# The high parts of K loaded by casting transfers on GpSimd's queue, in an attention and two-layer kernel on one core

## The chip, the cores and the metric

The kernel runs on one core of a Trainium2 chip. The metric is the device time of one execution in microseconds (us), as the median of several runs. Traces come from the hardware profiler, for one execution each.

## The reference

The program computes attention with pooled queries and feeds the result through two perceptron layers. Cut to what matters:

```
batch, n_heads, seq, head_dim = (2, 8, 1152, 64)
q_pool = q.reshape(B, H, S // 2, 2, D).mean(axis=3)
scores = scale * np.matmul(q_pool, k.transpose(0, 1, 3, 2))      # 576 x 1152 a head
attn = softmax(scores); x = np.matmul(attn, v)                   # 16 heads
x -> (1152, 512)
h = x @ w_in; g = softplus(h); x = g @ w_out                     # 512 -> 2048 -> 512
xn = rmsnorm(x); silu(xn @ w_gate) * (xn @ w_val) @ w_out        # 512 -> 1536 -> 512
```

All inputs and outputs are 32-bit floats. The change touches only how K comes to the score product.

## The kernel before

TensorE multiplies operands of a rounded 32-bit type (fp32r) in one pass. To keep the precision of the product, Q and K are each split into a high part, the value rounded to fp32r, and a low part, the value minus its high part; scores are sums of products of the parts.

The 16 heads are worked as eight pairs, `pb` 0 to 7. For each pair `prep` loads raw K of both heads, transposed, into the tile `kr`: 128 partitions (64 of the first head, 64 of the second) by 1152 positions. From `kr` it makes three things:

- `kk` of each head (two tiles, A and B): the high part of the head on 64 partitions and its low part on the other 64. The high part is one cast of 64x1152 (line 635), on VectorE or ScalarE; the low part is three subtractions of 64x384 (line 638), on VectorE or GpSimd, each of which reads `kr` and the high part.
- `kh` of the pair: the high part of both heads, one cast of 128x1152 (line 646). It serves the pair's last score product, for the last 64 rows of both heads at once.

Pair 0 (`first`) does the casts in three pieces of 384 positions, as they land. `kk` has two sets of tiles, for even and odd pairs, so that a pair's tiles are free once the pair two before has done its last scores. `kr` and `kh` have one tile each: `kr` is loaded anew when all its readers are done, and `kh` is written anew when the last scores of the pair before have read it.

Q goes beside it: the two halves that are pooled are summed into `qs` (`sum_q`, on VectorE or, after pair 0, on GpSimd), rounded to `qhA` or `qhB` (`round_q`, VectorE or ScalarE), and the low parts `qlA` and `qlB` and `qm` come from VectorE.

Per pair there are five row blocks `x`, four of 128 rows and one of 64. For each, `qk` puts scores into PSUM `s` (line 677), VectorE takes the maximum (`nm`, line 691), ScalarE the exponentials and their sums (`p`, line 693), TensorE transposes `p` through the PSUM tile `t` (line 712) and VectorE or ScalarE copies it to `pt` (helper lines 334 and 336), and TensorE multiplies with V (line 755). In pairs 1 to 6, block `x` = 1 is transposed by VectorE and 16 small transfers on SyncE's queue instead (lines 733 and 738). Beside attention, the first weights of the perceptron layers are decoded and split on ScalarE, VectorE and GpSimd (tiles `areaKF`, `areaKR`).

The order on each engine is written by a planner, `Plan`. Every `op` has options (an engine and a cost in us each), the buffers that it reads and writes, and `lat`, the time from the end of a transfer's issue to its landing. The order on TensorE is that of the program. `run` is a list scheduler: of the operations that could start first it takes the one that is due first, with its cheapest engine, and each engine's queue is then in the order of planned starts. A queue is worked strictly in order, so an instruction that waits holds back those behind it. Loads go on SyncE's queue (`load`). In the planner `dve(n, True)` is VectorE's fast copy, and `port` marks operations that it keeps apart from GpSimd's.

Of the kernel before, what the change touches and what calls it, by code (L numbers as in the profile page):

```python
# [21 lines left out]
B, H, S, D = 2, 8, 1152, 64  # L22
# [14 lines left out]
KB = S // N  # L37
# [43 lines left out]
class Plan:  # L81
# [68 lines left out]
    def op(self, opts, fn, r=(), w=(), lat=0.0, after=(), hurry=0.0):  # L150
        o = Op()
        o.fn, o.opts, o.lat, o.hurry = fn, opts, lat, hurry
        o.deps, o.after, o.succ = set(), set(after), []
        o.n = len(self.ops)
        for keys, writes in ((r, False), (w, True)):
            for b, part in keys:
                assert b.live, "a freed buffer"
                o.deps |= self.before(b, part, writes)
        for keys, writes in ((r, False), (w, True)):
            for b, part in keys:  # L160
                (b.writers if writes else b.readers).setdefault(part, []).append(o)
                if not b.ops or b.ops[-1] is not o:
                    b.ops.append(o)
        o.deps.discard(o)
        self.ops.append(o)
        if opts[0][0] == "PE":
            self.pe.append(o)
        return o
# [106 lines left out]
def dve(n, fast=False, psum=False):  # L275
    t = 0.157 + n / (1920 if fast else 960)
    return ("DVE", t) if psum else ("DVE", t, 1)


def act(n, sbuf=True):  # L280
    return "ACT", n * 0.00096 + 0.15 if sbuf else n * 0.00085 + 0.155


def pool(n):
    return "POOL", 0.05 + n * 0.00275
# [3 lines left out]
def body(ctx: ExitStack, tc: tile.TileContext, kT, qT, v, w1, w1o, wg, wv, w2o, rg, outM, outR):  # L289
    nc = tc.nc  # L290
# [3 lines left out]
    op = plan.op  # L294
# [32 lines left out]
    def ring(which, tag, shape, dtype=F32, bufs=1):  # L327
        b = plan.ring(tag, bufs, sb(which, tag, shape, dtype, bufs))
        owned[which].append(b)
        return b  # L330

    def copy(e, out, in_):
        if e == "ACT":
            nc.scalar.copy(out, in_)  # L334
        else:
            engines[e].tensor_copy(out, in_)  # L336
# [6 lines left out]
    def load(out, src, kb, w, queue="SP", lat=2.2, hurry=0.0):  # L343
        q = nc.sync if queue == "SP" else nc.scalar
        o = op([(queue, 0.6 + max(0, kb / 220 - 0.6))], lambda e: q.dma_start(out=out(), in_=src), w=w, lat=lat, hurry=hurry,
               after=issued[queue][-1:] if len(issued[queue]) < 10 else ())
        issued[queue].append(o)
        return o
# [195 lines left out]
    for z in range(2):  # L544
        for h in range(2):
            c = NF * P + (D if h == 0 else 0)
            op([dve(D)], lambda e, b=qx[z][h][0], c=c: copy(e, b()[:, c:c + D], zero), w=[(qx[z][h][0], "z")])
            r = slice(h * D, h * D + D)
            c = D - h * D
# [4 lines left out]
    def prep(pb):  # L554
        s = st[pb]
        n = PAIRS[pb][0] * H + 2 * PAIRS[pb][1]
        first = pb == 0
        s["kk"], s["v"] = [], []
        s["q"] = qx[pb % 2]
        kr = ring("e", "kr", [P, S])  # L560
        qr, qs = [], []
        kcuts = [(c, slice(c * N, c * N + N), N) for c in range(KB)]
        f = NF * P

        def load_q(h, c, queues=("SP", "SP")):
            cut = slice(0, 2 * P) if c == 0 else slice(2 * P, 2 * SQ) if c == 1 else slice(0, 2 * SQ)
            for z in range(2):
                parts = [(qr[h], (x, z)) for x in range(2) if c in (x, None)]
                load(lambda z=z: qr[h]()[z * D:z * D + D, cut], qT[n + h][:, cut], (cut.stop - cut.start) // 4, parts, queues[z], hurry=0.0 if first else EARLY)

        for h in range(2):
            qr.append(ring("a", "p1", [P, 2 * SQ], F32, 2) if first and h else ring("e", "qr", [P, 2 * SQ]))
            qs.append(ring("a", "O", [P, SQ], F32, 2) if first and h else ring("e", "qs", [P, SQ]))
        if first:
            load_q(0, 0, ("SP", "ACTQ"))
        pairs = kT[n:n + 2].rearrange("a d s -> (a d) s")
        if first:
            for c, cut, m in kcuts:
                load(lambda cut=cut: kr()[:, cut], pairs[:, cut], 192, [(kr, c)], "SP" if c else "ACTQ", (2.0, 3.1, 2.7)[c])
            load_q(1, 0)  # L580
        else:
            load(kr, pairs, 576, [(kr, None)], hurry=EARLY)
        for h in range(2):
            load_q(h, 1 if first else None)
            vt = ring("ea"[pb % 2], f"v{h}{pb % 2}", [P, CK, D])
            s["v"].append(vt)
            load(vt, v[n + h], 288, [(vt, None)])

        def round_q(h, key, x, m, i):
            qh, ql = s["q"][h]  # L590
            o = slice(x, x + m)
            op([dve(m, True), act(m)], lambda e: scale16(e, qh()[:, o], qs[h]()[:, i]), r=[(qs[h], None)],
               w=[(qh, k) for k in key])
            op([dve(m)], lambda e: nc.vector.scalar_tensor_tensor(
                out=ql()[:, o], in0=qs[h]()[:, i], scalar=0.0625, in1=qh()[:, o], op0=ALU.mult, op1=ALU.subtract),
               r=[(qs[h], None)] + [(qh, k) for k in key], w=[(ql, k) for k in key])

        def sum_q(h, part, a, m):
            o = slice(a, a + m)
            i = a if part == 0 else a + P  # L600
            j = i + (P if part == 0 else SQ - P)
            op([dve(m)] if first else [dve(m), pool(m)], lambda e: tt(
                e, qs[h]()[:, o], qr[h]()[:, i:i + m], qr[h]()[:, j:j + m], ALU.add), r=[(qr[h], (part, z)) for z in range(2)],
               w=[(qs[h], part)])

        kh = s["kh"] = ring("a", "kh", [P, S], F32R)

        def last_q(h):
            qh, low = s["q"][h][0], qm[pb % 2]
            x = f if h == 0 else f + D  # L610
            r = slice(h * D, h * D + D)
            op([dve(D, True), act(D)], lambda e: scale16(e, qh()[:, x:x + D], qs[h]()[:, f:]), r=[(qs[h], None)], w=[(qh, "e")])
            op([dve(D)], lambda e: nc.vector.scalar_tensor_tensor(
                out=low()[r, h * D:h * D + D], in0=qs[h]()[r, f:], scalar=0.0625, in1=qh()[r, x:x + D],
                op0=ALU.mult, op1=ALU.subtract), r=[(qs[h], None), (qh, "e")], w=[(low, ("e", h))])

        for h in range(2):
            kk = ring("ea"[pb % 2], f"kk{h}{pb % 2}", [P, S], F32R)
            s["kk"].append(kk)
            hi, lo = slice(h * D, h * D + D), slice(D - h * D, P - h * D)  # L620
            if first:
                sum_q(h, 0, 0, P)
                round_q(h, ("m0",), 0, P, slice(0, P))
                for c, cut, m in kcuts:
                    op([dve(m, True), act(m)], lambda e, kk=kk, hi=hi, cut=cut: copy(e, kk()[hi, cut], kr()[hi, cut]),
                       r=[(kr, c)], w=[(kk, ("h", c))])
                    op([dve(m)], lambda e, kk=kk, hi=hi, lo=lo, cut=cut: tt(
                        e, kk()[lo, cut], kr()[hi, cut], kk()[hi, cut], ALU.subtract),
                       r=[(kr, c), (kk, ("h", c))], w=[(kk, ("l", c))])
            else:  # L630
                sum_q(h, 0, 0, P)
                for x in range(2):
                    sum_q(h, 1, P + x * (SQ - P) // 2, (SQ - P) // 2)
                round_q(h, ("m0", "m1"), 0, f, slice(0, f))
                op([dve(S, True), act(S)], lambda e, kk=kk, hi=hi: copy(e, kk()[hi], kr()[hi]),
                   r=[(kr, None)], w=[(kk, ("h", c)) for c in range(KB)])
                for c, cut, m in kcuts:
                    op([dve(m), pool(m)], lambda e, kk=kk, hi=hi, lo=lo, cut=cut: tt(
                        e, kk()[lo, cut], kr()[hi, cut], kk()[hi, cut], ALU.subtract),
                       r=[(kr, None), (kk, ("h", c))], w=[(kk, ("l", c))])  # L640
        for h in range(2):
            if first:
                sum_q(h, 1, P, SQ - P)
                round_q(h, ("m1",), P, f - P, slice(P, f))
            last_q(h)
        op([dve(S, True), act(S)], lambda e: copy(e, kh(), kr()), r=[(kr, None)], w=[(kh, None)])
        s["den"] = ring("a", "den", [P, 2 * NF + 1], F32, 2)
        s["O"] = ring("a", "O", [P, SQ], F32, 2)

# [853 lines left out]
    for which, name in (("soft", "softplus"), ("silu", "silu_and_others")):  # L1503
        before = {"soft": "exp", "silu": "soft"}[which]
        first = op([("ACT", 1.3)], lambda e, name=name: nc.scalar.preload_act_table_set(name))
# [63 lines left out]
```

## Time and profile before

| | |
|---|---|
| median of three runs | 656.72 us (656.21 to 656.9) |
| the profiled execution's own time | 656.31 us |
| its span, first to last instruction | 654.5 us |
| mean granted clock of TensorE | 0.997 |

The execution's own time is that of the run in which the trace was taken; the span leaves out 1.8 us around the first and last instruction. Attention lies in the first 236 us or so of the span, the two perceptron layers behind it. In the rows, PE is TensorE's matmuls and PEld its weight loads, DVE is VectorE, ACT ScalarE, POOL GpSimd and SPq the issuing side of SyncE's queue. Instructions that only issue a transfer are not counted as busy time. L334 and L336 are one helper that copies or casts on ScalarE and on VectorE, and L339 is one that adds or subtracts, so that the tile's name tells what is done.

### The profile page before, as it was taken

The page shows a single profiled execution, that of the slowest core. Times are in us where ns is not written, and L with a number is a line of the kernel's source. Part 1 is how long each engine was busy: PE and PEld are TensorE (multiplying, and loading weights), DVE is VectorE, ACT ScalarE, POOL GpSimd, SP SyncE. Part 2 cuts the span into 40 slices and gives each one's busy share as a digit, 9 for nine tenths or more (in the row PEclk, how much of TensorE's full clock was granted, in tenths as well). Part 3 has the DMA queues.
Part 4 walks back from the last instruction along what each step waited for, and adds up shares of the span by engine and source line. Part 5 has one row for each costly group of instructions (what it writes and reads, how often), then busy time and mean ns, then how long its engine had stood idle before and what let it go on. Part 6 is the DMA issues. An engine that isn't in the chain of part 4 may idle for free.

```text
span 654.5 us, 11104 instructions
## 1 busy us (share of the span) xinstructions
PE 641.6 (98%) x4376; PEld 546.8 (84%) x4376; DVE 496.3 (76%) x741; ACT 399.4 (61%) x648; POOL 117.2 (18%) x131
## 2 busy tenths in 40 slices
PE   8999999999999999999999999999999999999997
PEld 7988889898998888888888888887788888888786
DVE  7888878898989877798877585669887787875320
ACT  4878788887887786556655654355464546563311
POOL 0442365445451310000000000000000100020000
PEclk8999999999999999999999999999999999999999
DMA  7643565656374530133231101300533231310102
GB/s 188 185 127 82 132 156 153 146 144 166 99 203 104 176 126 1 70 126 127 77 126 56 64 3 65 124 5 0 193 130 118 75 129 66 129 65 1 64 1 80
DMA packets 25026, 66.78 MB, mean 102 GB/s; under 512 B 5327, under 2 KB 6286, under 8 KB 24974
## 3 DMA queue, kind: packets, MB, share of 16 engines
q1 hardware_dynamic: 24462, 65.68, 33.0%
q8 instruction: 34, 0.56, 0.3%
q10 hardware_dynamic: 512, 0.40, 0.2%
q14 instruction: 18, 0.15, 0.1%
HBM read 56.59 MB, written 2.39 MB: 90 GB/s over the span
## 4 chain that ended last, share of the span: by engine, by line
PE 90%; DVE 5%; SPq 2%; DMA 1%; ACT 1%; issue 1%; ACTq 0%; DVEq 0%
PE s L870 24%; PE s L677 11%; PE t L755 10%; PE s L1371 9%; PE t L712 7%; PE t L870 4%; PE s L937 3%; PE s L938 3%; PE s L936 3%; PE t L1371 3%; PE t L957 2%; PE s L957 2%; PE t L983 2%; SPq L738 1%; DMA kr<-in_kT_dram 1%; PE s L983 1%
## 5 line engine op out<-in xcount | busy, mean ns | idle before, releaser
L691 DVE TENSOR_REDUCE nm<-s 128x1 f32<-128x1152 f32 x72 | 96.4, 1350 | 12.0 <-PE s L677 11.5
L693 ACT ACTIVATE p<-s,nm 128x1152 f32<-128x1152 f32 x72 | 88.0, 1223 | 17.8 <-DVE nm L691 15.6
L712 PE MATMUL t<-ident,p 128*128 128x128 f32 x468 | 70.4, 280 | 3.1 <-DVE pt L336 1.0
L334 ACT COPY pt<-t 128x512 f32<-128x512 f32 (+2 forms) x105 | 53.4, 523 | 24.7 <-PE t L712 20.6
L755 PE MATMUL t<-pt,v 128*64 128x128 f32 (+1 forms) x1224 | 67.0, 263 | 0.0
L334 ACT CAST areaKR<-areaKF 128x512 fp32r<-128x512 f32 (+1 forms) x56 | 48.7, 877 | 28.8 <-PE t L1371 17.0
L755 PEld LDWEIGHTS t<-pt,v 128*64 128x64 f32 x1224 | 59.6, 137 | 6.9 <-issue 5.8
L712 PEld LDWEIGHTS t<-ident,p 128*128 128x128 f32 x468 | 52.7, 140 | 14.7 <-issue 3.4
L870 PE MATMUL s<-areaMR,areaKR 128*128 128x512 f32 x192 | 48.5, 392 | 0.0
L339 POOL TENSOR_TENSOR kk<-kr,kk 64x384 fp32r<-64x384 f32 x40 | 40.8, 1045 | 39.2 <-ACT kk L334 36.5
L415 DVE SCALAR_TENSOR_TENSOR areaKF<-areaKF 128x1024 int32<-128x1024 int32 (+1 forms) x38 | 44.3, 1169 | 4.1 <-ACT areaKF L404 3.6
L870 PE MATMUL s<-areaKR 128*128 128x512 f32 x180 | 46.8, 398 | 0.1
L334 ACT CAST areaLR<-areaKF 128x1024 fp32r<-128x1024 f32 (+1 forms) x31 | 28.0, 910 | 26.1 <-PE s L1371 15.5
L339 DVE TENSOR_TENSOR areaKR<-areaKF,areaKR 128x1024 fp32r<-128x1024 f32 (+1 forms) x37 | 39.3, 1076 | 6.0 <-ACT areaKR L334 5.8
L339 DVE TENSOR_TENSOR areaKF<-areaKF 128x256 f32<-128x256 f32 (+1 forms) x92 | 41.2, 479 | 1.4 <-ACT areaKF L1010 0.4
L870 PEld LDWEIGHTS s<-areaMR,areaKR 128*128 128x128 f32 x192 | 35.4, 188 | 7.2
L404 ACT ACTIVATE areaKF<-areaKF 128x1024 f32<-128x1024 f32 (+1 forms) x38 | 39.8, 1053 | 0.3 <-DMA areaKF<-in_w_dram 0.3
L870 PEld LDWEIGHTS s<-areaKR 128*128 128x128 f32 x180 | 32.6, 188 | 7.2 <-ACT s L334 0.3
L336 DVE COPY pt<-t 128x512 f32<-128x512 f32 (+2 forms) x49 | 31.2, 650 | 9.3 <-PE t L712 8.5
L870 PE MATMUL s<-areaKR,areaLR 128*128 128x512 f32 x144 | 37.6, 400 | 0.5 <-DVE areaKR L339 0.5
L1072 POOL TENSOR_TENSOR n<-n,power 128x4 f32<-128x4 f32 (+1 forms) x3 | 3.1, 1029 | 175.1 <-DVE n L1070 175.1
L677 PE MATMUL s<-kk,qhA 128*128 128x384 f32 x120 | 31.3, 366 | 1.6 <-DVE kk L339 1.6
(269 smaller groups left out, 1431.0 us busy)
## 6 DMA issues: line engine op xcount, KB each, us to landing
areaKF<-in_w_dram SPq DMA_DIRECT2D x16, 512.0 KB, 4.2
areaKF<-in_w1o_dram SPq DMA_DIRECT2D x16, 512.0 KB, 4.4
qr<-in_qT_dram SPq DMA_DIRECT2D x28, 288.0 KB, 4.5
areaKF<-areaKF SPq DMA_DIRECT2D x96, 72.0 KB, 2.1
areaKF<-in_wg_dram SPq DMA_DIRECT2D x12, 512.0 KB, 3.9
areaKF<-in_wv_dram SPq DMA_DIRECT2D x12, 512.0 KB, 4.6
areaKF<-in_w2o_dram SPq DMA_DIRECT2D x12, 512.0 KB, 3.3
v<-in_v_dram SPq DMA_DIRECT2D x16, 288.0 KB, 3.6
```

Source lines behind the costliest of these rows:

```text
L334: nc.scalar.copy(out, in_)
L336: engines[e].tensor_copy(out, in_)
L339: engines[e].tensor_tensor(out=out, in0=in0, in1=in1, op=o)
L404: o = op([act(n)], lambda e, x0=x0, x1=x1: nc.scalar.activation(out=word(1, x0, x1).bitcast(F32), in_=word(1, x0, x1).bitcast(F32), scale= ...
L415: op([dve(n)], lambda e, x0=x0, x1=x1: nc.vector.scalar_tensor_tensor(out=word(1, x0, x1), in0=word(1, x0, x1), scalar=3, in1=word(0, x0, ...
L677: nc.tensor.matmul(sc()[:, c, :N], lhsT=q()[:, cut], rhs=k()[:, c * N:(c + 1) * N], start=(i == 0), stop=(i == len(todo) - 1))
L691: u["mx"] = op([dve(S, psum=True)], lambda e: nc.vector.tensor_reduce(out=nm(), in_=sc()[:, :, :N], axis=AX.XY, op=ALU.max, negate=True), ...
L693: o = op([("ACT", 1.42)], lambda e: nc.scalar.activation(out=pr(), in_=sc()[:, :, :N], func=AF.Exp, bias=nm(), accum_out=s["den"]()[:, col ...
L712: nc.tensor.transpose(t()[:, i * P:(i + 1) * P], pr[:, c * P:(c + 1) * P], ident)
L755: nc.tensor.matmul(t()[h * D:h * D + D, :n], lhsT=s["v"][h]()[:, c, :], rhs=rhs, start=(c == 0), stop=(c == CK - 1))
L870: nc.tensor.matmul(bank(), lhsT=a(k), rhs=b(k), start=start and k + i == 0, stop=stop and k + i == 3, skip_group_check=seeded)
L1371: nc.tensor.matmul(out[m](), lhsT=w, rhs=g(), start=j + i == 0, stop=last and j == js[-1] and i == 2)
```

## The change

For pairs 1 to 7, the high part of each head's `kk` and the pair's `kh` are no longer cast from `kr`. Each is read again from K in main memory by a transfer on GpSimd's queue, whose destination has the type fp32r, so that the transfer casts. The planner is told 1.2 us on GpSimd for the issue and 4.0 us until it lands. `kr` is still loaded for the low parts, which still wait for the high parts. Pair 0 keeps its casts.

```diff
@@ -632,8 +632,8 @@
                 for x in range(2):
                     sum_q(h, 1, P + x * (SQ - P) // 2, (SQ - P) // 2)
                 round_q(h, ("m0", "m1"), 0, f, slice(0, f))
-                op([dve(S, True), act(S)], lambda e, kk=kk, hi=hi: copy(e, kk()[hi], kr()[hi]),
-                   r=[(kr, None)], w=[(kk, ("h", c)) for c in range(KB)])
+                op([("POOL", 1.2)], lambda e, kk=kk, hi=hi, h=h: nc.gpsimd.dma_start(out=kk()[hi], in_=kT[n + h]),
+                   w=[(kk, ("h", c)) for c in range(KB)], lat=4.0)
                 for c, cut, m in kcuts:
                     op([dve(m), pool(m)], lambda e, kk=kk, hi=hi, lo=lo, cut=cut: tt(
                         e, kk()[lo, cut], kr()[hi, cut], kk()[hi, cut], ALU.subtract),
@@ -643,7 +643,10 @@
                 sum_q(h, 1, P, SQ - P)
                 round_q(h, ("m1",), P, f - P, slice(P, f))
             last_q(h)
-        op([dve(S, True), act(S)], lambda e: copy(e, kh(), kr()), r=[(kr, None)], w=[(kh, None)])
+        if first:
+            op([dve(S, True), act(S)], lambda e: copy(e, kh(), kr()), r=[(kr, None)], w=[(kh, None)])
+        else:
+            op([("POOL", 1.2)], lambda e: nc.gpsimd.dma_start(out=kh(), in_=pairs), w=[(kh, None)], lat=4.0)
         s["den"] = ring("a", "den", [P, 2 * NF + 1], F32, 2)
         s["O"] = ring("a", "O", [P, SQ], F32, 2)
```

## Rows read from the trace of the kernel before

**Rows 1.** The page, busy time, share of the span and instructions of each engine.

```profile
PE 641.6 (98%) x4376; PEld 546.8 (84%) x4376; DVE 496.3 (76%) x741; ACT 399.4 (61%) x648; POOL 117.2 (18%) x131
```

**Rows 2.** Windows, us busy (instructions): PE, PEld, DVE, ACT, POOL; clock, DMA share, GB/s.

```profile
87.00:115.00 28.00, 27.79 (x303) 25.42 (x302) 21.75 (x28) 23.23 (x40) 14.39 (x16) 1.00 0.62 160
115.00:143.20 28.20, 27.88 (x302) 25.36 (x302) 24.68 (x35) 23.74 (x40) 12.02 (x14) 1.00 0.55 137
143.20:171.30 28.10, 27.97 (x304) 25.34 (x302) 25.01 (x34) 23.85 (x42) 15.53 (x17) 1.00 0.54 140
171.30:199.50 28.20, 27.88 (x302) 25.31 (x302) 24.75 (x36) 22.64 (x39) 16.08 (x18) 1.00 0.65 175
...
240.00:654.50 414.50, 408.41 (x1968) 335.76 (x1966) 291.35 (x449) 209.31 (x320) 21.61 (x17) 1.00 0.21 75
```

**Rows 3.** Waits of all engines, 18 to 236 us: us, times, longest.

```profile
PEld t L712 <- DVE pt L336: 2.4, 6, 0.6
...
PE t L712 <- DVE pt L336: 1.0, 3, 0.3
...
PEld t L712 <- ACT O L334: 0.5, 1, 0.5
...
PE t L712 <- ACT pt L334: 0.2, 1, 0.2
```

**Rows 4.** Tile kr: ns minimum/median/maximum, first and last start, forms.

```profile
L339 POOL TENSOR_TENSOR kk<-kr,kk x40: 992/1004/1457, 25.0 to 198.5; 64x384 fp32r<-64x384 f32 x40
L334 ACT CAST kk<-kr x16: 508/1150/1157, 4.9 to 193.4; 64x1152 fp32r<-64x1152 f32 x13, 64x384 fp32r<-64x384 f32 x3
L345 SPq DMA_DIRECT2D kr<-in_kT_dram x9: 327/515/1237, 1.4 to 185.1; - x9
...
L334 ACT CAST kh<-kr x6: 1157/1161/1167, 37.0 to 205.9; 128x1152 fp32r<-128x1152 f32 x6
L336 DVE CAST kh<-kr x2: 750/886/1021, 17.5 to 61.6; 128x1152 fp32r<-128x1152 f32 x2
...
DMA to landing us min/median/max: 3.2/4.3/5.6
```

**Rows 5.** Timeline, raw K of pair 6: start us, us, engine, line, operation, tiles.

```profile
157.47 0.52 SPq L345 DMA_DIRECT2D kr<-in_kT_dram  x1
...
168.79 0.74 DVE L336 CAST kk<-kr 64x1152 fp32r<-64x1152 f32 x1
...
169.76 5.53 POOL L339 TENSOR_TENSOR kk<-kr,kk 64x384 fp32r<-64x384 f32 x5 [2.25 <-PE t L712]
...
176.99 0.77 PE L677 MATMUL s<-kk,qhA 128*128 128x384 f32 x3
```

**Rows 6.** The page, transfers by source: count, KB each, median us to landing.

```profile
v<-in_v_dram SPq DMA_DIRECT2D x16, 288.0 KB, 3.6
```

**Rows 7.** Timeline around the load of raw K in pair 2's time.

```profile
71.33 0.47 SPq L345 DMA_DIRECT2D kr<-in_kT_dram  x1
...
76.34 1.15 ACT L334 CAST kk<-kr 64x1152 fp32r<-64x1152 f32 x1 [1.01 <-DMA kr<-in_kT_dram]
77.39 1.21 ACT L693 ACTIVATE p<-s,nm 128x1152 f32<-128x1152 f32 x1
...
78.75 0.44 PE L677 MATMUL s<-kk,qhB 128*128 128x384 f32 x1 [0.67 <-ACT p L693]
```

**Rows 8.** Timeline, end of pair 3 and first scores of pair 4.

```profile
115.32 2.93 POOL L339 TENSOR_TENSOR kk<-kr,kk 64x384 fp32r<-64x384 f32 x3 [3.46 <-ACT kk L334]
...
115.89 0.68 PE L677 MATMUL s<-kh,qm 128*128 128x384 f32 x3
...
118.60 1.07 POOL L339 TENSOR_TENSOR qs<-qr 128x224 f32<-128x224 f32 x2 [0.35 <-POOL kk L339]
...
121.31 0.69 DVE L594 SCALAR_TENSOR_TENSOR qlB<-qs,qhB 128x512 fp32r<-128x512 f32 x1
...
122.62 0.77 PE L677 MATMUL s<-kk,qhB 128*128 128x384 f32 x3
```

## The prediction

> **What bounds the kernel now.** The profile's busy line comes first: TensorE is busy for 98% of the span, VectorE for 76%, ScalarE for 61%, GpSimd for 18% [rows 1]. A change that only lightens VectorE and ScalarE can therefore win nothing but the time in which TensorE waits for them. The change touches attention alone, which lies in the first 236 us or so, and the windows by pair show how close to full TensorE is there: in pairs 3 to 6 it is busy 27.79 to 27.97 us of 28.0 to 28.2, while VectorE has 21.75 to 25.01 us and ScalarE 22.64 to 23.85 us of work in the same time [rows 2]. A matmul's end is modelled, so part of that busy time may be hidden waiting, but not much. After 240 us the two perceptron layers run with TensorE busy 408.41 us of 414.5 [rows 2]; nothing of K is left there, and I cost that stretch at no change.
>
> The waits of TensorE in attention (18 to 236 us) are the second view. Its matmul row waits visibly six times over for ScalarE or VectorE, 3.3 us in all, from 1.0 us for copies out of PSUM by VectorE down to 0.2 us [rows 3]. Its weight-load row, which shows idle time that the modelled ends hide, names the same two engines in six larger entries (copies of transposed scores 2.4 and 0.7, exponentials 2.3 and 1.1, copies of the output 0.9 and 0.5): 7.9 us [rows 3]. These 3.3 and 7.9 us bound what faster help could return.
>
> **What the casts cost, and what goes.** Seven pairs lose three casts each. The rows of the tile that holds raw K give them: 13 casts of 64x1152 on ScalarE at 1.15 us (15.0 us), one on VectorE at 0.74 [rows 5]; six of 128x1152 on ScalarE at 1.16 us (7.0 us), and of VectorE's two the one at 1.02 us (the 0.75 us one belongs to pair 0, which keeps it) [rows 4]. Sum: 22.0 us off ScalarE and 1.8 us off VectorE, 23.8 us, or 3.4 us a pair.
>
> They are not on TensorE's path by themselves. What they do is fill slots: in pairs 3 to 6 the two engines together have 189.7 us of work in 2 x 112.5 us, which leaves 35.3 us free [rows 2]. Without the casts (4 x 3.4 = 13.6 us) 48.9 us are free. I take the waits of TensorE for these engines to shrink as the free time grows, to 35.3/48.9 = 72% of what they are. That gives back 28% of 3.3 us = 0.9 us at the least and 28% of 7.9 us = 2.2 us at the most; I take the middle, **1.5 us**. This proportion is an estimate of mine, not something a row shows.
>
> **What the casts held up.** The low part of K (raw minus high, three pieces a head, mostly on GpSimd at 1.0 us each [rows 4]) had to wait for a cast to find a slot. In pair 5's time raw K for pair 6 was issued at 157.47, the first cast came at 168.79, and the five subtractions on GpSimd ended at 175.3, 1.7 us ahead of the pair's first score matmul at 176.99 [rows 5]. Afterwards the high part can be fetched as soon as the tile of two pairs ago has been read, some 20 us before it is needed; a load of 576 KB lands in 3.2 to 5.6 us [rows 4] and one of 288 KB in 3.6 us [rows 6], so the transfer is hidden by that lead. If it were not, each head's subtractions would start up to 5.6 us later than raw K, and the 1.7 us of margin would go. The tile of raw K is also free sooner: its last reader was the whole-pair cast, which could come after the next pair had begun. In pair 2 the load of raw K stood in SyncE's queue until 71.33, its cast ran 76.34 to 77.49, an exponential queued behind it on ScalarE, and TensorE stood still for 0.67 us until 78.75 [rows 7]. That stall should go; it is one of the 3.3 us above and is not counted again.
>
> **What comes in.** 21 issues on GpSimd's queue. The trace has no transfer issued there, so the price is bounded by rows: the same tile's issues on SyncE take 0.33 to 1.24 us [rows 4], and GpSimd's own work over the same 64x1152 elements takes 2.93 us in three pieces (115.32, [rows 8]). I take 1.24 us, the longest issue of this tensor, since an issue writes no 64x1152 elements. That is 3.7 us a pair (1.0 to 8.8 us) on an engine with 12.0 to 16.1 us of counted work in 28 [rows 2]; even the dear end fits, at 24.9 us, so by throughput it costs nothing. What hides it is GpSimd's idle time; where it would not be hidden is the first rival below.
>
> Traffic: two heads of 288 KB and one pair of 576 KB are 1,152 KB (1.18 MB) a pair, 42 GB/s over 28 us, on 137 to 175 GB/s that now take 0.54 to 0.65 of the transfer engines [rows 2]. At the same rate per share that adds 0.13 to 0.17, up to about 0.8. Nothing saturates; I cost it at zero, and at the landing times above if transfers bunch.
>
> Waits: the transfer for a whole pair's high part may start only when the last score matmuls of the pair before have read the old one (115.89 plus 0.68, [rows 8]). It stands in GpSimd's queue, and what is queued behind it are the sums of Q for the next pair and the subtractions for raw K. It is needed a pair later, some 27 us.
>
> **Sum.** 656.31 us for the profiled execution, minus 1.5, plus 0: 654.8 us. The median of the runs is 656.72, 0.41 above that execution, so the forecast is **655.2 us**, 0.23% below the median.
>
> **A rule against it.** GpSimd shares a port to the memory with VectorE; here a subtraction of K that takes GpSimd 0.99 us at best takes up to 1.46 us [rows 4]. The Trainium skill (SBUF — State Buffer, section "SBUF: two separate sides", the box on DVE blocking a DMA) says that a transfer issued from GpSimd has its descriptors written by that engine, which is locked out while VectorE runs a fast-mode copy: 620 ns alone became about 3100 ns there. No run here shows that yet. By it an issue would take 3.1 us, an estimate from that page, 9.3 us a pair, and the sum would still hold by throughput, but the next rival would decide.
>
> **Rivals.**
>
> *GpSimd comes late with the sums of Q* (slower). At the end of each pair three transfers become ready at once: the next pair's whole high part and both heads for the pair after. In pair 3 that moment is 116.57. GpSimd then sums Q at 118.60, VectorE finishes the last sum, rounds, and ends the low part at 122.00; TensorE uses it at 122.62 [rows 8]. So three issues have 2.03 us before the sums and 0.62 us of margin behind them: free up to 2.65/3 = 0.88 us each. At 1.24 us they make TensorE 1.07 us late, in six pairs 6.4 us; with the 1.5 us gained, 661.6 us. At 2.93 us each it is 6.1 us a pair and the time near 690 us. For it: the sums now start as soon as their tile is free. Against it: the planner charges 1.2 us for the issue, may place the sums on VectorE, and the subtractions that fill 115.32 to 118.25 now [rows 8] move to an earlier time. It decides as soon as an issue takes more than the 1.2 us which the order was planned with and the sums stand behind it.
>
> *The casts were in the gaps* (no change). ScalarE and VectorE wait for TensorE far more than it waits for them, the planner fills gaps with casts, and most of TensorE's waits are the latency of maximum, exponential and transposition, which stays: 656.3 to 657.0 us. For it: six visible waits in 218 us; against it: the stall at 78.75 is behind a cast.
>
> *More comes back.* Raw K leaves SyncE's queue ahead of the small transfers, low parts are ready well ahead, and the copies out of PSUM are spread over two less busy engines, so that half to three quarters of the 7.9 us return, 4 to 6 us: 650.7 to 652.7 us. For it: the 7.9 us; against it: TensorE is nearly full.
>
> **How the numbers follow.** Forecast 0.40 (its own range 654.5 to 655.8, 2.2 and 0.9 us below the median), rival one 0.25, rival two 0.23, rival three 0.12. From no change a measurement of this kernel can tell about 0.2%, 1.3 us. The forecast lies across that bound: two thirds of it below (0.28), one third within (0.12). Faster: 0.28 + 0.12 = 0.40. Same: 0.12 + 0.23 = 0.35. Slower: 0.25. The range takes in rival two, most of rival three, and rival one with the issue at 1.24 us, but not its dear end: 651.5 to 662 us.
>
> **What would show it.** Right: no casts from raw K after pair 0; ScalarE about 22 us less busy; 21 issues on GpSimd of 1.0 to 1.3 us; subtractions ending over 5 us ahead of the next pair's scores; the PSUM copies' and exponentials' entries in the waits of TensorE shorter, and pairs 3 to 6 at 27.6 to 27.9 us. Wrong: issues of 2 us or more with subtractions or sums of Q behind them, TensorE waiting for the low part of Q or K at a pair's start, pairs over 28.5 us; or pairs of the same length as now in spite of the free engines.

## The result, and the profile after

The changed kernel takes **664.88 us** (median of four runs, 664.01 to 666.36) against 656.60 for the kernel before on the same chip. The ratio is 1.0126, 95% interval [1.011, 1.0142]: slower by 8.3 us, where 1.5 us less were forecast, and above the range, which ended at 662. The profiled execution took 664.01 us.

The busy line and the transfer rows of the page of the changed kernel (count, KB each, median us from issue to landing):

```profile
PE 642.0 (97%) x4376; PEld 546.9 (83%) x4376; DVE 494.3 (75%) x735; ACT 383.3 (58%) x637; POOL 127.5 (19%) x148
...
q1 hardware_dynamic: 24462, 65.68, 32.4%
q0 software_dynamic: 2128, 8.26, 5.4%
...
kk<-in_kT_dram POOLq DMA_DIRECT2D x14, 288.0 KB, 6.9
...
kh<-in_kT_dram POOLq DMA_DIRECT2D x7, 576.0 KB, 5.1
```

ScalarE has 16.1 us less to do than in [rows 1], VectorE 2.0. So the casts are gone, and yet TensorE, with the same work, needs 7.7 us more of span.

The same windows as [rows 2], moved with the pairs (pairs 3 to 6, then the stretch behind attention):

```profile
89.60:119.80 30.20, 27.86 (x304) 25.44 (x303) 22.28 (x31) 20.38 (x38) 19.09 (x23) 1.00 0.79 176
119.80:150.60 30.80, 28.38 (x302) 25.27 (x302) 26.81 (x37) 19.50 (x36) 11.36 (x15) 1.00 0.71 178
150.60:178.60 28.00, 27.79 (x303) 25.35 (x302) 24.18 (x31) 23.67 (x44) 17.71 (x21) 1.00 0.71 183
178.60:207.50 28.90, 28.19 (x304) 25.36 (x303) 24.93 (x32) 20.27 (x38) 13.03 (x17) 1.00 0.79 200
247.80:662.20 414.40, 408.28 (x1968) 335.72 (x1966) 291.81 (x449) 209.45 (x320) 22.00 (x17) 1.00 0.20 75
```

The perceptron stretch is the same to 0.1 us. The loss lies in attention, and not evenly: two pairs last 30.2 and 30.8 us, the others about as long as before. The share of the transfer engines has risen by 0.14 to 0.17, to 0.71 to 0.79, as the prediction added up.

From TensorE's timeline of every kernel, the start of the first score matmul and the length of each pair, from the last score matmuls (kh) of the pair before to its own, in us. Each row is the one execution that was traced; for tiny and half that was the slowest of ten (659.25 and 660.21 us, where their medians are 657.99 and 658.41). The experiments below say what each kernel is.

| kernel | first score | pair 0 | 1 | 2 | 3 | 4 | 5 | 6 | 7 |
|---|---|---|---|---|---|---|---|---|---|
| before | 6.10 | 26.06 | 26.94 | 28.82 | 27.97 | 28.21 | 28.09 | 28.20 | 32.87 |
| changed | 8.98 | 26.65 | 26.95 | 27.94 | 30.16 | 30.84 | 27.98 | 28.84 | 32.70 |
| tiny | 7.16 | 26.66 | 26.92 | 27.96 | 28.13 | 29.02 | 28.82 | 28.67 | 32.71 |
| half | 7.25 | 26.67 | 26.96 | 27.95 | 29.73 | 29.29 | 27.99 | 28.65 | 32.68 |
| pair1_cast | 5.67 | 26.16 | 26.95 | 35.72 | 29.01 | 31.54 | 29.27 | 28.38 | 32.56 |
| tiny1 | 5.83 | 27.06 | 26.95 | 27.97 | 28.97 | 32.51 | 29.23 | 30.11 | 32.56 |
| before_bytes2 | 5.90 | 26.28 | 26.95 | 31.58 | 27.99 | 29.99 | 28.11 | 28.88 | 32.86 |
| in_place | 5.89 | 26.07 | 26.94 | 29.04 | 28.20 | 33.10 | 28.07 | 28.71 | 32.85 |

The changed kernel against before: +2.88 at the start, +0.59 in pair 0, -0.88 in pair 2, +2.19 in pair 3, +2.63 in pair 4, +0.64 in pair 6, the rest within 0.2; in all 7.8 us. Three places make it up, and one gives something back (pair 2, whose stall of 0.67 us at 78.75 in [rows 7] is gone).

**The start.** ScalarE and TensorE of the kernel before:

```profile
4.95 1.58 ACT L334 CAST kk<-kr 64x384 fp32r<-64x384 f32 x3 [0.94 <-DMA kr<-in_kT_dram]
...
6.10 0.44 PE L677 MATMUL s<-kk,qhA 128*128 128x384 f32 x1 [0.58 <-DVE kk L339]
```

GpSimd, ScalarE and TensorE of the changed kernel:

```profile
1.43 1.26 POOL L635 DMA_DIRECT2D kk<-in_kT_dram  x2
...
7.89 0.51 ACT L334 CAST kk<-kr 64x384 fp32r<-64x384 f32 x1 [4.37 <-DMA kr<-in_kT_dram]
...
8.98 0.41 PE L680 MATMUL s<-kk,qhA 128*128 128x384 f32 x1 [3.09 <-DVE kk L339]
```

Nothing holds pair 1's two transfers, so GpSimd issues them at 1.43 us, beside the first pieces of raw K, which pair 0 needs at once. Those land late, and the first scores start 2.9 us later.

**Pair 3.** GpSimd, SyncE, VectorE, TensorE:

```profile
91.52 0.61 POOL L649 DMA_DIRECT2D kh<-in_kT_dram  x1 [1.05 <-PE s L680]
92.12 1.06 POOL L635 DMA_DIRECT2D kk<-in_kT_dram  x2
...
90.49 1.40 SPq L345 DMA_DIRECT2D qr<-in_qT_dram  x2
...
99.37 0.39 DVE L339 TENSOR_TENSOR qs<-qr 128x224 f32<-128x224 f32 x1 [3.34 <-DMA qr<-in_qT_dram]
...
102.56 0.28 DVE L783 TENSOR_SCALAR sums<-t 9x128 f32<-9x128 f32 x1
...
102.90 0.66 PE L715 MATMUL t<-ident,p 128*128 128x128 f32 x4 [2.02 <-DVE sums L783]
```

The last scores of pair 2 free kh and two kk at once; three transfers, 1.18 MB, go out within 1.7 us, on the heels of two loads of Q. The second of these, issued at 91.42, lands at 99.25, 7.8 us later. VectorE, which takes its instructions in order, stands at the sum of Q for 3.34 us; behind it are two maxima and the copy of the sums out of PSUM, which TensorE waits for. **Pair 4** is the same with another small transfer: `sums` may be written anew only when the transfer of the row from it (4.5 KB, issued at 126.11) has landed, and that took 6.7 us behind the burst at 122.95. ScalarE's copy waits for `sums`, and TensorE for the copy. The chain that ended last, VectorE, ScalarE and TensorE:

```profile
126.11 6.73 DMA row<-sums
...
132.93 0.28 DVE L783 TENSOR_SCALAR sums<-t 9x128 f32<-9x128 f32 x1 [2.13 <-DMA row<-sums]
...
133.24 0.27 ACT L334 COPY pt<-t 128x128 f32<-128x128 f32 x1 [2.36 <-DVE sums L783]
...
133.56 0.66 PE L715 MATMUL t<-ident,p 128*128 128x128 f32 x4 [2.10 <-ACT pt L334]
```

The times from issue to landing of the transfers that touch `row` (us, minimum, median, maximum; before, then changed) show the same. The profile matches a landing only to the loads back from `row` to `rdb`, not to the writes of `row`:

```profile
DMA to landing us min/median/max: 2.7/3.6/4.1
...
DMA to landing us min/median/max: 2.5/3.4/9.6
```

The median has hardly moved; the tail has. TensorE met two late transfers of this kind, the 7.8 and 6.7 us of pairs 3 and 4.

### The profile page after: what moved, and what is told of

Same layout as the page of the kernel before. It is cut to its first block, busy times and chain, and to the rows that moved or that the text cites. A ratio compares the mean times of both kernels' runs of the same rounds, so it can differ in the third digit from the quotient of the medians.

```text
span 662.2 us, 11133 instructions
## 1 busy us (share of the span) xinstructions
PE 642.0 (97%) x4376; PEld 546.9 (83%) x4376; DVE 494.3 (75%) x735; ACT 383.3 (58%) x637; POOL 127.5 (19%) x148
## 3 DMA queue, kind: packets, MB, share of 16 engines
q1 hardware_dynamic: 24462, 65.68, 32.4%
q0 software_dynamic: 2128, 8.26, 5.4%
## 4 chain that ended last, share of the span: by engine, by line
PE 83%; DVE 6%; DMA 5%; issue 2%; ACT 1%; SPq 1%; POOL 1%; ACTq 0%; DVEq 0%; POOLq 0%
PE s L873 24%; PE s L1374 9%; PE s L680 9%; PE t L758 8%; PE t L715 6%; PE t L873 4%; PE s L940 3%; PE s L941 3%; PE s L939 3%; PE t L1374 2%; PE t L960 2%; DMA qr<-in_qT_dram 2%; PE s L960 2%; PE t L986 2%; PE s L986 1%
## 5 line engine op out<-in xcount | busy, mean ns | idle before, releaser
L334 ACT COPY pt<-t 128x512 f32<-128x512 f32 (+2 forms) x113 | 57.8, 523 | 38.7 <-PE t L715 26.1
L336 DVE COPY pt<-t 128x512 f32<-128x512 f32 (+2 forms) x41 | 26.3, 655 | 8.3 <-PE t L715 7.6
```

## The experiments

Two theories stood against each other. A: the bytes of the new transfers hold up the small loads of SyncE's queue, which share the transfer engines. B: the loss comes from something else that changed with them, GpSimd's issues and their waits, or the new order that the planner makes. Each kernel was run beside the kernel before on its chip (medians of that 656.8 to 657.5 us); ratios are to it.

### How many bytes

**tiny** keeps the changed kernel's order, issues and waits, and transfers 32 of 1152 columns (0.23 MB):

```
-nc.gpsimd.dma_start(out=kk()[hi], in_=kT[n + h])
+nc.gpsimd.dma_start(out=kk()[hi, :32], in_=kT[n + h][:, :32])
+nc.gpsimd.memset(kk()[hi, 32:].bitcast(F32), 0.0)
...
```

> Leaves out 1120 of the 1152 columns of each casting transfer and fills them with zeros on GpSimd, so the scores of pairs 1 to 7 are wrong; planned order, issues and waits are those of the changed kernel, the bytes fall from 8.26 MB to 0.23 MB. Theory A (the transfers crowd SyncE's loads on the shared transfer engines: 2.9 us at the start, 2.0 us at 100.9, 2.1 us at 131.5 of the changed kernel): those three stalls go and the time is 655 to 658 us. Rival B (the new order of the queues, or GpSimd's issues in front of other work): the time stays within 1.5 us of 664.9 us, more if the fills on GpSimd cost.

Measured 657.99 us, 1.0014 [1.0004, 1.0025]: 6.9 us of the 8.3 go with the bytes. The number of packets stays, so it isn't that. GpSimd's queue in the pages of the changed kernel and of tiny (packets, MB, share of 16 engines):

```profile
q0 software_dynamic: 2128, 8.26, 5.4%
...
q0 software_dynamic: 2128, 0.23, 0.5%
```

Of the late start 1.06 us is left (7.16 for 6.10), and no run says why.

**half** has 576 for 32 in that edit (4.13 MB).

> The changed kernel with half the columns in each of its 21 transfers (576 of 1152), the other half filled with zeros by GpSimd instead of the rounded high part; orders, issues and waits are otherwise those of the change. 4.13 MB instead of 8.26; the same with 0.23 MB took 657.99 us, and all of it 664.88. If each byte costs the same, 661 to 662 us. If what counts is how long one burst holds up the load behind it (a wait starts only once the load is later than the work ahead of it covers), the cost bends: 657.5 to 660. If the bytes are not the cause, 664 to 666.

Measured 658.41, 1.0014 [1.0001, 1.0026], in the range of the bend. **double** issues each transfer twice (16.5 MB).

> Each casting transfer is issued twice (42 issues, 16.5 MB), all else as in the changed kernel. Theory A: a burst at a pair's end is twice as long (about 10 us), so loads behind it land some 5 us later: the start at 12 us or more, stalls of up to 7 us in several pairs, 675 to 700 us. Rival by GpSimd's issues (0.54 to 0.61 us each, 11.8 us more in all): at most 668 us.

Measured 738.36, 1.1238 [1.1207, 1.127], above the range given for A. TensorE's clock adds to it: from 88 to 144 us TensorE, busy for 36.36 of the 56 us, was granted 0.85 of the full 2.4 GHz on average. So 0.23, 4.13, 8.26 and 16.5 MB cost 0.1, 0.1, 1.3 and 12.4%: not a price per byte. By the medians half a burst stays within the slack of the loads behind it, and a whole one doesn't. It is not always so: in the traced execution of half, the slowest of ten, TensorE still waits 1.56 us for `sums` at 100.78, where the changed kernel waits 2.02.

### Which transfers

**heads_only** transfers into kk alone, **pairs_only** into kh alone (the other keeps its casts), each with a new plan.

> Only the heads' high parts are transferred; the pair's is cast as before. Theory A: half of the bytes at a pair's end are gone, the start is late by 2.9 us as in the changed kernel, at most one of the later stalls is left: 659 to 662.5 us. Rival B, by GpSimd's issues (14 of 21 left): 662 us or more, with the stalls in other places.

> Only the pair's high part is transferred (576 KB at a pair's end); the heads are cast as before. Theory A: no transfer at the start, so the first scores are at 6.1 us, and at most one later stall of 2 us: 656 to 659 us. Rival B: 7 of 21 issues, 658 to 660 us, with the loss spread over the pairs' ends.

Measured 664.82, 1.0121 [1.0106, 1.0136], and 659.17, 1.0035 [1.0022, 1.0048]. heads_only lies above A's range, in B's: its first scores are as late as forecast (9.07), but pairs 4 and 5 lose 1.5 and 2.6 us. By the trace these are not the bytes: TensorE waits 0.85 us for VectorE's subtraction at 128.51 and 1.61 us for its copy of O at 174.43, and the chain that ended last holds no transfer there, only VectorE's own queue. pairs_only lies just above A's range and in B's; its longest wait of TensorE, 1.68 us for an exponential at 121.32, comes back below in two other plans.

**pair1_cast** casts pair 1's heads as before, to regain the start:

```
+if pb == 1:
+    op([dve(S, True), act(S)], lambda e, kk=kk, hi=hi: copy(e, kk()[hi], kr()[hi]), ...)
+else:
     op([("POOL", 1.2)], lambda e, kk=kk, hi=hi, h=h: nc.gpsimd.dma_start(out=kk()[hi], in_=kT[n + h]), ...)
```

> Pair 1's two heads are cast as before, all other high parts are transferred. Theory A: nothing is in the way of the first loads, the first scores start at 6.1 us in place of 9.0, and the time is 661 to 662.5 us, with the two later stalls left. Rival B: the start is one of the engines' own, 9 us as now, and the time is 664 to 666 us.

Measured 669.54, 1.0195 [1.0178, 1.0212], above both ranges. The start came back (5.67) and more was lost: under its plan the burst at pair 2's start meets a load of Q issued at 61.02, and pair 2 lasts 35.72 us. Part of that is TensorE's clock, which stood at its lower level from 73.11 to 79.94 us (more on this under before_bytes2). SyncE, VectorE and TensorE of this kernel:

```profile
61.02 0.50 SPq L345 DMA_DIRECT2D qr<-in_qT_dram  x1
...
70.59 0.29 DVE L339 TENSOR_TENSOR qs<-qr 128x128 f32<-128x128 f32 x1 [6.15 <-DMA qr<-in_qT_dram]
...
74.01 1.11 PE L719 MATMUL t<-ident,p 128*128 128x128 f32 x4 [4.98 <-DVE sums L787]
```

**tiny1** is pair1_cast with tiny's 32 columns.

> The kernel whose transfers carry 32 of 1152 columns (657.99 us; GpSimd fills the other columns with zeros in place of the rounded high part), with pair 1's heads cast as before, so that nothing is transferred at the start. What is left of the change is the casts that are gone, less GpSimd's fills. If the casts removed are worth the 1.5 us of the prediction once the bytes are gone, 655 to 656 us. If they lay in gaps and are worth nothing, 656.5 to 658.

Measured 663.54, 1.0094 [1.008, 1.0108], outside both. The bytes account for 6.0 us of pair1_cast, and pair 2 is back at 27.97; but 6 us are left that are no bytes. TensorE's row of tiny1:

```profile
121.69 1.09 PE L727 MATMUL t<-ident,p 128*128 128x128 f32 x8 [1.68 <-ACT p L708]
```

pair1_cast has the same wait of 1.68 us at 128.43, and both wait 1.10 us for the copy of O a pair later. A stall that stays to the hundredth when the bytes go, and GpSimd fills tiles in one and not in the other, belongs to the order both share. These two make 2.8 of the 6 us; the rest lies in the plan, the fills or the clock (at its lower level from 122.91 to 126.33 in tiny1), and is not separated. So a new plan can cost some microseconds without any bytes. With tiny, the changed kernel's own plan, its casts gone and GpSimd's fills added come to 1.1 us net.

### Where the transfers stand

**start_wait** puts pair 1's two transfers behind GpSimd's first sum of Q:

```
+held, behind = [st[1]["hi", h] for h in range(2)], False
 for o in plan.order():
+    if o in held and not behind:
+        continue
     o.fn(o.eng)
+    if o.eng == "POOL" and o not in held and not behind:
+        behind = True
+        for x in held:
+            x.fn(x.eng)
```

> The changed kernel with one move: pair 1's two transfers stand behind GpSimd's first sum of Q (about 20 us) in place of the start; the order of every other queue is the same. Theory A (bytes crowd the loads): pair 0's first scores start at 5.7 to 6.1 us in place of 9.0, the two later stalls stay, and the time is 661 to 662.5 us; the same transfers may make something near 22 us late instead. Rival B (order): no change from 664.9 us.

Measured 665.0, 1.0129 [1.0098, 1.0159], the time that B gave, but not by B's way: the start came back by 2.8 us, and pair 0 then lasts 4.2 us longer. The moved transfers stood in front of the next load of Q, TensorE waits 2.64 us for it at 32.24 (0.54 in the changed kernel), and its clock then falls to its lower level from 33.45 to 36.86.

**staggered** holds each transfer with a one-column mark by ScalarE, so that they are spread over the pair; **told** only has the planner reckon 8 us for loads of Q and for the row of sums. Both are planned anew.

> All 21 transfers, each held by a mark of one column that ScalarE writes when a given maximum of scores is done, so that no two start together and none at the start or at a pair's end (21 more writes of some 0.2 us on ScalarE). Theory A: start at 6.1 us, no stall over 1 us behind a load of SyncE; 655 to 659 us. Rival B (GpSimd's issues, order): still above 662 us.

> The changed kernel with the planner told 8 us in place of 2.2 and 4.0 for the landing of Q's loads after pair 0 and of the row of sums, so that VectorE's queue should not have the waiting sums ahead of maxima. Theory A with both halves (a late load, and a queue worked in order behind it): the start stays at 9.0 us, the two stalls of 2 us go: 659.5 to 661.5 us. If lateness alone did it, wherever the sums stand: 664 us or more.

Measured 667.11, 1.0151 [1.0129, 1.0172], and 670.8, 1.0198 [1.0162, 1.0235]. Neither helped: staggered took the time of its rival B, told that of lateness alone. Neither tests this cleanly, since new waits came. In staggered the start is back (6.23) and no wait of TensorE of 1 us or more is left behind a load, but one of 2.95 us has come (for an exponential, at 208.58, behind sums of Q and transpositions in VectorE's queue); told moved many instructions, and waits of 2.85 and 1.89 us came at 50 and 65 us.

**behind_q** holds every transfer until GpSimd's next sum of Q has been issued, or a reader needs it; **behind_q1** does the same to pair1_cast.

```
+if o in held:
+    waiting.append(o)
+    continue
...
+if o in sums_of_q and o.eng == "POOL":
+    for x in waiting:
+        x.fn(x.eng)
```

> The changed kernel with its plan; only each transfer on GpSimd's queue is put behind the next sum of Q that GpSimd does, so that it starts when the loads of Q it would crowd have landed. The same bytes. If the place of the bursts, in front of loads that somebody needs soon, is what costs, the waits of 2.0 us at 103 and 2.1 us at 133 go, and pair 1's start gives 2.8 us back (of which the earlier trial gave 2.6 away again): 657.5 to 662 us. If the bytes cost wherever they are put, as in the trial that spread them, 663 to 667.

> The kernel in which pair 1's heads are cast as before (669.54 us), with each transfer that is left put behind the next sum of Q that GpSimd does. If the place of the bursts is what costs, the stall of 4.98 us at 74 goes, and of those of 1.7 and 1.1 us after it a part: 661 to 664. If the bytes cost wherever they are put, 667 to 671.

Measured 680.23, 1.0315 [1.026, 1.037], and 683.71, 1.0389 [1.0348, 1.0431]: outside all ranges, the worst but double. VectorE and TensorE of behind_q:

```profile
146.08 0.29 DVE L336 COPY O<-t 128x128 f32<-128x128 f32 x1 [6.67 <-POOL areaKF L339]
...
249.45 0.79 PE L680 MATMUL s<-kh,qm 128*128 128x384 f32 x3 [3.87 <-DMA kh<-in_kT_dram]
```

GpSimd, whose own queue had stood 9.74 us for a load of Q until 132.54, comes 6.67 us late with an operation that VectorE waits for; and in the last pair, which no sum of Q follows, kh itself is late. Moving the bursts by hand isn't tested cleanly by this, since it makes GpSimd's own queue late.

### The same bytes in the order of before

These leave the planned order of the kernel before untouched. **before_bytes** keeps all casts and adds casting transfers into kk, which the casts overwrite: two of 288 KB for pair 1, and two of 576 KB for each later pair, as many bytes there as in the change; **before_bytes2** does so for pairs 2 to 7 alone.

```
 for o in order:
+    for key in [x for x in free if not free[x]]:
+        ...
+        nc.gpsimd.dma_start(out=st[pb]["kk"][h](), in_=st[pb]["pairs"])
     o.fn(o.eng)
```

> The kernel before with all its casts and its planned order, to which GpSimd adds transfers of the same kind and of 7.7 MB in all into the tiles kk, as soon as each is free; the casts overwrite them 10 us and more later. What moves bytes is added, nothing is removed, and no engine's order is planned anew. If the bytes in front of SyncE's loads are the cause, this loses as the change did: 661 to 668 us, with DVE's sums of Q and the row of sums late after a burst. If the new planned order is the cause, and the bytes only share it, it stays within 656 to 658.

> The kernel before with casts and order kept and the added transfers of pairs 2 to 7 alone (7.1 MB): no transfer at the start. The same with pair 1's two transfers took 668.55 us, of which its first scores were 6 us late. If the bursts at the turns of the pairs cost by themselves, 660 to 664; if the loss lay in the start alone, 656 to 658.

Measured 668.55, 1.0166 [1.0139, 1.0193], and 663.61, 1.0086 [1.0065, 1.0108], the first just above the range for the bytes, the second in it. Nothing is removed, and GpSimd's added issues are all that is new in any queue; none of them waits. The bytes cost 6 us, and 5 more at the start. Pair 2 of before_bytes2 can be laid beside [rows 7] line by line (SyncE of before, then SyncE, ScalarE and TensorE of before_bytes2):

```profile
65.49 5.68 SPq L738 DMA_DIRECT2D areaKF<-areaKF  x8
...
65.74 7.14 SPq L739 DMA_DIRECT2D areaKF<-areaKF  x8
73.04 0.47 SPq L345 DMA_DIRECT2D kr<-in_kT_dram  x1
...
77.64 1.15 ACT L334 CAST kk<-kr 64x1152 fp32r<-64x1152 f32 x1 [2.28 <-DMA kr<-in_kT_dram]
78.69 1.21 ACT L694 ACTIVATE p<-s,nm 128x1152 f32<-128x1152 f32 x1
...
80.06 1.00 PE L678 MATMUL s<-kk,qhB 128*128 128x384 f32 x3 [1.94 <-ACT p L694]
```

SyncE's eight issues ahead of raw K take 7.14 us where they took 5.68, so raw K is issued 1.71 us later than in [rows 7]; the cast starts 1.30 later, the exponential behind it 1.30, and TensorE waits 1.94 instead of 0.67, 1.27 more. From the cast on, the delay is handed on almost whole.

That is not all that this wait costs. Pair 2 is 2.76 us longer, and TensorE's clock takes the other half. Windows of before_bytes2, laid out as [rows 2]:

```profile
78.00:80.00 2.00, 0.12 (x3) 0.00 (x0) 2.00 (x4) 2.00 (x4) 1.08 (x2) 1.00 0.23 48
80.00:82.00 2.00, 1.95 (x7) 1.85 (x8) 0.56 (x1) 1.98 (x4) 2.00 (x3) 0.61 0.20 72
82.00:84.00 2.00, 2.00 (x10) 2.00 (x9) 1.36 (x1) 1.40 (x3) 1.92 (x4) 0.53 0.38 91
```

From 78 to 80 us TensorE was busy for 0.12 of the 2 us; from 80.45 to 83.86 its clock was granted at 0.5, 1.2 GHz of 2.4, and a score matmul of 128x384 took 522 ns in place of 334. The same matmuls fall behind by a further 1.47 us. The changed kernel's clock stayed at 1.00 after its waits of 2.02 and 2.10 us, so its own loss there is the waits alone.

**in_place** replaces the 18 casts of pairs 2 to 7 by their transfers in that same order; **kh_in_place** and **kk_in_place** replace only those into kh or kk.

```
+gone = {x[2] for x in free}
...
+    if o not in gone:
         o.fn(o.eng)
```

> The kernel before in its own planned order; only the casts of the high parts of pairs 2 to 7 (18 of them, some 20 us on ACT and DVE) are replaced, each by a transfer that GpSimd issues once the tile is free. 7.1 MB, as in the trial that adds them and keeps the casts (663.61 us). The difference between the two is the worth of the casts by itself, without a new plan: 663 to 664.5 if they lay in gaps, 662 to 663 if they are worth the 1.3 us that the prediction gives for six pairs, under 660 if as much as doubling them cost (15 us for 23.8) comes back in part.

> As the one above, with the six casts into kh alone replaced (3.5 MB, 6 to 7 us of casts); heads are cast as before. Half of the bytes cost about 1 us in the changed kernel (658.41). If bursts of this size are covered, and the casts are worth something, 655.5 to 657 us; if neither, 657.5 to 660.

> As the first, with the twelve casts into kk of pairs 2 to 7 alone replaced (3.5 MB, 12 to 14 us of casts). A kk has a whole pair of time before it is needed and its cast stands in front of an exponential in the stall at 78.75 of before. If bursts of this size are covered, 655 to 657 us; if not, 658 to 661.

Measured 662.41, 1.0078 [1.0064, 1.0093]; 659.06, 1.0022 [1.001, 1.0035]; 658.16, 1.0013 [1.0001, 1.0024]. in_place against before_bytes2, which moves as many bytes (in fewer, larger transfers), is an estimate of the worth of the casts: 1.2 us by the medians, 0.5 by the ratios, in intervals that overlap (in_place lies in the range that goes with 1.3 us). Half the bytes cost 1.9 and 1.0 us, in the ranges given for bursts that are not covered; neither version beats the kernel before. GpSimd, SyncE, VectorE and TensorE of in_place show the mechanism without any new plan:

```profile
121.87 1.15 POOL L1543 DMA_DIRECT2D kk<-in_kT_dram  x2
...
121.95 1.14 SPq L345 DMA_DIRECT2D qr<-in_qT_dram  x2
...
130.46 0.29 DVE L339 TENSOR_TENSOR qs<-qr 128x128 f32<-128x128 f32 x1 [3.17 <-DMA qr<-in_qT_dram]
...
131.01 2.11 PE L756 MATMUL t<-pt,v 128*64 128x64 f32 x36 [2.35 <-DVE O L336]
```

Behind this wait, too, TensorE's clock is at its lower level, from 131.14 to 134.55 us, which costs about 1.6 us more; together they make most of the 4.9 us by which pair 4 is longer.

**casts_twice** does each cast of before twice in a row:

```
-lambda e, kk=kk, hi=hi: copy(e, kk()[hi], kr()[hi])
+lambda e, kk=kk, hi=hi: [copy(e, kk()[hi], kr()[hi]) for _ in range(2)]
...
```

> The kernel before with each cast of a high part of pairs 1 to 7 done twice in a row on the engine that has it: 23.8 us more on ACT and DVE, no byte more on a queue. If a cast is worth what the prediction took it for (1.5 us for all of them), 657.5 to 659.5; if they lie in gaps, 656.5 to 657.3; over 661 would mean that their removal was worth more than was forecast, and that the change lost more elsewhere.

Measured 672.62, 1.023 [1.0213, 1.0247]. 23.8 us of casts added cost 15 us (3.0 of them by the clock, behind two waits), while their removal is worth an estimated 0.5 to 1.2. ScalarE and TensorE of this kernel show one place:

```profile
203.60 4.69 ACT L334 CAST kk<-kr 64x1152 fp32r<-64x1152 f32 x4
208.32 0.59 ACT L334 COPY pt<-t 128x512 f32<-128x512 f32 x1
208.93 1.22 ACT L693 ACTIVATE p<-s,nm 128x1152 f32<-128x1152 f32 x1
...
210.29 1.11 PE L712 MATMUL t<-ident,p 128*128 128x128 f32 x4 [2.27 <-ACT p L693]
```

Two heads' casts, twice each, run for 4.69 us in front of a copy and an exponential, and TensorE waits 2.27 us for that; half as long, as in the kernel before, no such wait stands there. So a time over 661 does not mean what the expectation took it for: doubling work doesn't measure what its removal returns.

## Why the prediction was wrong

**The casts' worth: not contradicted, not shown.** They left (ScalarE 16.1 us less busy, VectorE 2.0, where 22.0 and 1.8 were named; the engines share other work anew). 1.5 us was taken for seven pairs, 1.3 for six; in_place against before_bytes2 gives 0.5 to 1.2, which can't be told from zero. The rule of proportion behind the 1.5 us was not tested. The stall at 78.75 went, as forecast. The prediction's six visible waits are six entries with eight waits; their sum of 3.3 us stands.

**The low parts: earlier, as forecast, but not all.** For pair 6 GpSimd's subtractions end at 179.58, 4.9 us ahead of the first scores at 184.45, where it was 1.7 before; one piece that VectorE took ends only 0.1 us ahead.

**GpSimd's issues: too dear.** Taken at 1.24 us, they took 0.52 to 0.76. The Trainium skill (SBUF — State Buffer, section "SBUF: two separate sides") gives about 3.1 us for a transfer beside a VectorE copy. The issue rows, 0.76 us at most, show nothing of the kind; that figure is for the transfer and not the issue, and no run separates such a delay within the landings of the new transfers, 4.6 to 10.8 us.

**Traffic: the step that failed.** "Nothing saturates; I cost it at zero, and at the landing times above if transfers bunch." The average was right, 0.71 to 0.79 for "up to about 0.8" (pair by pair its sum gives a rise of 0.16 to 0.17; the 0.13 takes the share of one pair with the rate of another). But a kernel meets traffic in bursts. By the rows of the page, the new queue moved 8.26 MB in 5.4% of 662.2 us, 231 GB/s, so a pair's 1.18 MB is an estimated 5.1 us of work for all transfer engines together. And the landing times were applied to the new transfers alone, which had 20 us to spare; what had no time to spare were the loads of Q and the row of sums in SyncE's queue beside them (+2.19 and +2.63 us), and at the start pair 0's first loads (+2.88). tiny takes nearly all of the cost away and keeps order, issues and packets (it adds GpSimd's fills); before_bytes and before_bytes2 bring such a cost into the kernel before, whose casts and planned order stay. The Trainium skill states the ground for it (DMA: Bandwidth & Descriptors, section "Issuing engines are not separate DMA queues"): transfers started from any engine run on the same 16 transfer engines and interleave. The traces agree: 7.8 us for a load of Q that has a median of 4.4.

**The first rival** named the moment, the end of a pair with three transfers ready at once, and the sums of Q behind it, and its 661.6 us came nearer than the forecast. Its mechanism was not what happened: it needed 0.88 us an issue, and in pair 3 GpSimd had issued all three by 93.2 and then waited 6.24 us for Q like VectorE. **The second**, no change, fits the casts' worth as well as the forecast does. **The third**, more coming back, has nothing for it: tiny, without the bytes, is no faster than before.

**What stays open.** The 0.6 us each in pairs 0 and 6 are nearly all there in tiny and half too (26.66 and 28.67 us), so they are not the bytes; whether order or issues make them was not separated. Whether some placement of whole bursts is harmless isn't settled: the attempts moved the collision, or made GpSimd late, or changed the plan. No run moves the same bytes without the cast, or on SyncE's queue, so whether the cast or GpSimd's queue adds to the cost is open.

## What to carry to other kernels

When work moves from an engine to a transfer, look not at the mean share of the transfer engines but at the moment of the burst: which small loads are issued within some 5 us of it, who waits for them, and what stands behind that wait in an in-order queue. Look at the maximum of the landing times, not the median. Adding the new transfers to the old kernel, or keeping the new kernel and shrinking its transfers, separates bytes from order. After a long wait, look at TensorE's granted clock before the whole loss is put down to the wait.

## What the runs showed of the hardware

- GpSimd's transfers took more of the transfer engines for each byte than SyncE's: 231 GB/s of their busy time against 306 (65.68 MB in 32.4% of 662.2 us). The cast is not the whole reason, since all of them cast: into 64 partitions it was 200 (kk_in_place, 3.54 MB in 2.7% of 656.0 us), into 128 it was 257 (kh_in_place, 3.54 MB in 2.1% of 655.0 us).
- In the plan of the changed kernel the cost of the bytes bends: by the medians 0.23 and 4.13 MB cost 1.1 us each, 8.26 MB 8 us, and 16.5 MB 82 us with TensorE's clock lowered as well.
- A wait of TensorE can cost a second time. After waits of 1.94 us (before_bytes2, 80.06) and 2.35 us (in_place, 131.01) TensorE's clock was granted at 1.2 GHz for a stretch, and TensorE lost a further 1.5 and 1.6 us. Not every wait does this: the 1.68 us of tiny1 were followed by such a stretch, the 1.68 us of pair1_cast and the 2.10 us of the changed kernel were not.
- In tiny, VectorE's rounding copy of 128x512, 0.40 us at best, took 2.60 us while GpSimd filled tiles, and TensorE waited 1.09 us behind it. VectorE and GpSimd of tiny:

```profile
147.92 2.60 DVE L665 TENSOR_SCALAR qhB<-qs 128x512 fp32r<-128x512 f32 x1
...
149.17 1.07 POOL L591 MEMSET kk<- 64x1120 f32 x1
```
